# Routing turns and global outputs on 128 partitions, and the router's logits from one operand of both gate parts

## The chip, the cores and the metric

The kernel runs on one core of one Trainium2 chip. The metric is the device time of one execution, in microseconds (us); lower is better. Three executions of the kernel before took 813.44, 819.76 and 821.40 us, median 819.76.

## The reference

Three stages follow each other, in float32. Attention has 4 batches of 8 heads with 64 columns each: 32 global queries see all 544 keys (32 global, 512 local), and 512 local queries see the global keys and those at most 32 places away. The result, 4 x 544 = 2176 tokens of 512 columns, goes through a channel mix: each token is mixed with the one before it by `mu_k` and by `mu_r`, then `k = relu(xk @ w_k)`, `y = sigmoid(xr @ w_r) * (k*k @ w_v)`. Last comes a mixture of 8 experts:

```
logits = y @ w_gate                    # 8 columns
local  = sigmoid(y @ w_local)          # 1 column
e[s]   = argmax(logits[s]) if s == 0 or local[s] < 0.5 else e[s-1]
out[s] = softmax(logits[s])[e[s]] * (relu(y[s] @ w1[e[s]]) @ w2[e[s]])
```

The choice of an expert can be carried on from token to token within a batch, so it is a scan along the tokens.

## The kernel before

Phase 1 makes attention, channel mix and routing; phase 2 runs the experts. Most products are made with both operands split in two parts, an upper one and a rest (`mm3`, lines 19 to 24): upper by upper, upper by rest, rest by upper, three products added up in PSUM.

Attention goes by 16 units, pairs of heads, four to a batch. The first four units take float32 unsplit. `item` handles 128 local queries; `gitem` (lines 248 to 297) the 2 x 32 global ones of a unit. `gitem` ends with the products into `avg` (64 partitions x 128), a copy by ScalarE to `og` (line 287), a turn (a transpose on TensorE, that is a product with the identity `ident`) of the 64 x 128 values into `avt` (line 290), and two small copies by VectorE to `xT` (line 294), from which the channel mix reads.

The channel mix goes by nine groups of tokens, eight of two tiles of 128 tokens and one of one tile: 17 tiles. `run` (line 503) gives out the products `psk`, `psr` and `psv`. For each tile, `logits` (line 540) then makes four turns (`psy`), splits them in two parts `yT`, and multiplies with the gate: `s.g` holds `w_gate` (8 columns), `w_local` (1 column) and a column of zeros, halved, in an upper and a lower part, each 128 x 4 x 10 (`load_consts`, line 376). Four chunks of three products are 12 products into `psl`, 10 partitions x 128 tokens. ScalarE copies them to `lt` (10 x 128, line 560), TensorE turns them into `pslt` (128 x 10, line 564), VectorE copies them to `L` (line 567).

For each group, `route` (line 577) finds the expert of each token. It turns the codes of the tokens into a row on one partition (`psr1`, line 596), scans along the row (`row`, 1 x 256, line 600), turns the row back, tile by tile (`psc`, 1 x 128 to 128 x 1, line 609), and goes on on 128 partitions: counts, places in the experts' lists, and the lists (`psL`).

What sets the order: `Sched` (line 40) plans phase 1 when the program is built. Each stream of work yields steps with an engine, an assumed time (`yield op("P",.67,...)`: TensorE, 0.67 us), places to take and to leave, and a priority; instructions are given out in the order in which the steps start in that plan. The framework then orders the instructions by a simulated timeline of its own, so that the 12 products of one tile can stand apart in the trace. In the last groups some products for the first expert (`ahead`, line 791) are tied behind numbered steps of the last tile's routing (`step`, `order`, lists `ND` and `V7`). Phase 2 has a fixed order by hand.

At the start GpSimd fills constants and the tiles that must hold zeros (`pl`, `pg`, lines 97 and 98), before its first copies for attention (line 175).

Of the kernel before, what the change touches and what calls it, by code (L numbers as in the profile page):

```python
# [14 lines left out]
NEG=-1e9  # L15
FRESH=-1.08674975e-07  # the largest float32 z with 1/(1+exp(-z)) < 0.5 in float32
LEAST=float(np.array(0x38000000,np.int32).view(np.float32))  # the upper word of 2**-127 in float64, read as a float32

def mm3(nc,out,wh,wl,xh,xl,first,last,order=None):
    """out += w^T x with both operands split in two 12 bit parts"""  # L20
    i=nc.tensor.matmul(out,wh,xh,start=first,stop=False)  # L21
    if order: order(i)
    nc.tensor.matmul(out,wh,xl,start=False,stop=False)  # L23
    return nc.tensor.matmul(out,wl,xh,start=False,stop=last)  # L24


# order of the work: priorities of streams (the lower, the more urgent)
N0=3; PE0=-1.5; PC=-1; PW=1.5; PV=2; PM=0.5
NF=4  # the first pairs of heads, taken in float32 as it is
EV={"kn":"A","qn":"D","g":"D",0:"A",1:"A",2:"A",3:"A"}  # what empties their products' places  # L30
LN=12 ; PL=5  # parts of the experts' weights that are split in phase 1, and from which on GpSimd does it
GA=6; PA=6  # the group after which the first expert's first tile is closed, and the urgency of its work
ND=[k for k,n in enumerate([1, 5, 5, 11, 3, 4, 6, 16]) for _ in range(n)]  # how many of that tile's products follow each step of the last tile's routing
V7=[1,1,2,2,3,3,3,3]  # steps of the routing before the last tile's products
PP=(0,0,0,1,0,0,0,1); TW=(1,1,1,(2,4,6),3)  # parts of weights that GpSimd splits; where others go within a window of one tile
NR=4; NP=4  # places
FX=(1,3,5,7); FW=(2,4,6); NW=(2,3); NST=2  # where other work goes within a window; more stages for loads
LAT=0.2; DLAT=2.1; SLACK=dict(P=0.15,A=0,D=0,G=0)  # from an engine's end to the next step's start, and a load's
def op(e,d,need=(),free=(),when=None): return e,d,need,free,when
def wait(f): return "",0.0,(),(),f  # L40
class Sched:
    """The order in which the engines' instructions are given out. Streams of work are generators:
    each yields its next step (engine, time, places it takes, places it leaves, condition) and gives the
    step's instructions out when it is resumed, which is when the engine is free, the stream's step
    before is through and the places are there; of the streams that could go, the most urgent goes."""
# [7 lines left out]
    def one(s):  # L53
        """starts a step, if one can start now"""
        for x in sorted(s.L,key=lambda x:(s.t<x[3]+(SLACK.get(x[2][0],0) if x[4] else 0),x[0])):
            e,d,need,free,when=x[2]
# [20 lines left out]
class Pools:  # L77
    """a pool for the places of one tag and one for the others"""
# [4 lines left out]
class Attn:  # L83
    """attention by pairs of heads. The products of the first units, for whose time the tensor engine has
    nothing else to do, take float32 as it is; those of the others take it in two parts"""
    def __init__(s,tc,ident,mask,q_l,k_l,v_l,q_g,k_g,v_g,xT,sb,ps):
# [8 lines left out]
        s.pg=sb.tile([64,608],F32,name="pg",bufs=1)  # L95
        nc.vector.memset(s.gn,0.0)
        for t in s.pt_: nc.gpsimd.memset(t,0.0)
        nc.gpsimd.memset(s.pg,0.0)
        s.V={}; s.nat=set(); s.vnat=set(); s.T={}; s.sdone={}; s.vdone={}; s.odone={}
    def places(s,t):  # L100
        """of every other of the first units, in a tile that is filled later"""
        s.kwe=t[:,:896].rearrange("p (w i c) -> p w i c",w=1,i=4); s.gTe=t[:,896:992].unsqueeze(1); s.qTe=t[:,1024:1536].unsqueeze(1)
    def early(s,u): return u<NF
    def parts(s,u): return ((0,0),) if s.early(u) else ((0,0),(0,1),(1,0))
    def split(s,u,engine,out,x,place,d):
        """x to out, or to the two parts of it"""
# [53 lines left out]
    def prep(s,u,name):  # L160
        """transposed and split q or k of a pair of heads"""
# [33 lines left out]
    def item(s,u,i):  # L195
        """a block of local queries of a pair: its keys are the 32 before it, its own, the global ones
        and the 32 after it; the first block has none before it and the last one none after"""
# [27 lines left out]
        for c in range(2):  # L225
            # the second time with 32 of the first, for which v has zeros
            for h in range(2):
                nc.tensor.transpose(pt[:,c,h],p[:,h,c*96:c*96+P],s.ident)  # L228
# [15 lines left out]
    def weights(s,u):  # L244
        """a place for transposed weights or their parts"""
        return [s.sb.tile([P,2,256],F32 if s.early(u) else F32R,tag=t,name=t,bufs=2) for t in ("ph","plo")[:2-s.early(u)]]
    def v(s,u,w,i,c): return s.V[u][0][:,i,c] if s.early(u) else s.V[u][i//2][:,w,i%2,c]
    def gitem(s,u):
        """the global queries of a pair"""
# [36 lines left out]
        og=s.sb.tile([64,P],F32,tag="og",name="og",bufs=1)  # L286
        nc.scalar.activation(og,o,AF.Copy)
        yield op("P",.06,("av",))
        t=s.ps.tile([P,512],F32,tag="av",name="avt",bufs=1)[:,:64]
        nc.tensor.transpose(t,og,s.ident[:64,:64])  # L290
# [31 lines left out]
def band(nc,const):  # L322
    """0 for the keys in reach of a query of a block, NEG for the others"""
    m=const.tile([P,224],F32,name="mask")
    nc.gpsimd.memset(m,0.0)
    def keep(lo,hi,base,cm,step):
        # keeps 0 where base+cm*p+step*c >= 0
# [5 lines left out]
class Mix:  # L333
    """channel mix of groups of tokens, their router's logits and their places in the experts' lists"""
    def __init__(s,tc,ident,const,wsb,place,early,sb,ps,xT,mu,wk,wv,wr,gate,y):
# [7 lines left out]
        # places of the weights as they come: of other weights and of the router's operands, which are used later  # L343
# [7 lines left out]
    def consts(s,const):  # L351
# [11 lines left out]
        for b in range(NB):  # L363
            # 1 where p+128*c == 544*b
# [3 lines left out]
        # column m sums the rows p < m  # L368
# [3 lines left out]
        # of the first expert without its first tile  # L372
        s.up=t([P,E],"up"); nc.gpsimd.memset(s.up,float(P-1)); nc.gpsimd.memset(s.up[:,0:1],-1.0)
        s.last=t([1,1],"last"); nc.vector.memset(s.last,0.0)
        s.const=t
    def load_consts(s):
# [5 lines left out]
        g=t([P,4,10],"gf"); s.g=[t([P,4,10],f"g{w}",F32R) for w in range(2)]  # L382
# [4 lines left out]
        nc.vector.tensor_copy(s.g[0],g); nc.vector.tensor_sub(s.g[1],g,s.g[0].bitcast(F32))  # L387
    def weight(s,k,i):
        """loads 512 columns of a row, 128 of each of the four rows of wk or one row of the others,
        converts them from the bits of float64 and splits them"""  # L390
# [8 lines left out]
                # the least exponent is that of 2**-127 in float64  # L399
# [22 lines left out]
    def mixes(s,sched,groups):  # L422
        """mixed columns of tokens, split, group after group"""
# [42 lines left out]
    def kproc1(s,ps,kh,kl,b):  # L466
        """the same of a half of a group of one tile, which comes with the tokens on the partitions"""
# [28 lines left out]
    def run(s,sched,groups):  # L496
        """the groups of tokens one after another"""
# [41 lines left out]
    def logits(s,g,j,t,r,N):  # L539
# [14 lines left out]
        yield op("P",.67,(tag,),("yT",))  # L554
        ps=s.rps("psl",tag)
        for d in range(4): i=mm3(nc,ps[:10,:P],s.g[0][:,d],s.g[1][:,d],yT[0][:,d],yT[1][:,d],d==0,d==3)
        s.step(t,i)
        yield op("A",.16,(),(tag,))
        lt=s.sb.tile([10,P],F32,tag="lt",name="lt",bufs=1)
        nc.scalar.activation(lt,ps[:10,:P],AF.Copy)  # L560
        tag=s.ltag
        yield op("P",.05,(tag,))
        pl=s.rps("pslt",tag)[:,:10]
        s.step(t,nc.tensor.transpose(pl,lt,s.ident[:10,:10]))
        yield op("D",.1,(),(tag,))
        if g not in s.L: s.L[g]=s.sb.tile([P,N,10],F32,tag="L",name="L",bufs=2)
        nc.vector.tensor_copy(s.L[g][:,j],pl)
        yield wait(None)
        s.Lmade[g]+=1
    def routes(s,sched,groups):  # L570
        """the groups one after another; the last one's steps go before those that are left of the group before"""
# [5 lines left out]
    def route(s,g,tiles):  # L577
# [9 lines left out]
        # 8+8*token+8-expert at the tokens that choose, 0 at the others  # L587
# [11 lines left out]
        row=pool.tile([1,256],F32,tag="row",name="row",bufs=1)  # L599
# [4 lines left out]
        # p of each expert  # L604
        for j in range(N): nc.scalar.activation(ex[:,j],lg[:,j],AF.Exp,bias=nmx[:,j:j+1],scale=1.0,accum_out=sums[:,j:j+1])
        tag=s.rtag
        yield op("P",.05,(tag,))
        ps=s.rps("psc",tag)
        for j in range(N): i=nc.tensor.transpose(ps[:,j:j+1],row[:,j*P:(j+1)*P],s.ident[:1,:1])
# [413 lines left out]
```

## Time and profile before

| what | value |
|---|---|
| three timed runs | 813.44, 819.76, 821.40 us; median 819.76 |
| profiled execution | span 814.9 us from its first to its last instruction; the page gives no time of its own beside the span |
| TensorE (PE) busy | 747.8 us, 92% of the span, 4790 products |
| VectorE (DVE), ScalarE (ACT), GpSimd (POOL) busy | 525.7, 391.7, 388.1 us |
| chain that ended last | PE 69%, DVE 12%, DMA 8% |
| mean granted clock of TensorE | 0.956 of full |
| phase 1, phase 2 | to about 550 us; from there to the end |

How to read it: one execution was recorded. PE stands for products (MATMUL), PEld for loads of the operand that stays in the array. Products overlap, so the length of one (0.2 to 0.4 us) is not what it costs in a stream; that is the distance from its start to the start of the next. A line such as `L564` is a line of the kernel before, and `pslt<-ident,lt` names what is written and what is read. The form `10*128 10x10` reads: 10 rows by 128 columns in the array, 10 x 10 values stream through.

### The profile page before, as it was taken

What the parts mean: (1) busy time and instruction counts of PE and PEld (TensorE: products, weight loads), DVE (VectorE), ACT (ScalarE), POOL (GpSimd) and SP (SyncE); (2) the same over time, 40 slices, a digit from 0 to 9 for tenths busy, and PEclk for the clock granted to TensorE, in tenths of its full rate; (3) what the DMA queues carried; (4) which work ended last, traced back from release to release, by engine and by line L of the source; (5) the groups of instructions that cost most, each with busy time, mean ns of one, the idle gap of its engine ahead of it and who ended that gap; (6) DMA issues with size and microseconds to landing.
All of it is one profiled execution on the core that took longest, in us unless ns stands there. A gap on an engine that the chain in (4) does not pass through costs nothing.

```text
span 814.9 us, 14252 instructions
## 1 busy us (share of the span) xinstructions
PE 747.8 (92%) x4790; PEld 629.0 (77%) x4790; DVE 525.7 (65%) x1477; ACT 391.7 (48%) x978; POOL 388.1 (48%) x507
## 2 busy tenths in 40 slices
PE   6988899899999998999998999786899999999974
PEld 3655687798878877978887897565697999988963
DVE  6699889776695875786667845863473725536531
ACT  4787576663555644656544332213561615224420
POOL 6678868646153563462461412944462413324130
PEclk9997999999999999899998999978899999999988
DMA  6664241202102202111002200337684533518210
GB/s 151 168 183 147 74 113 54 76 22 54 35 15 76 50 13 70 44 27 50 23 14 99 96 27 27 117 121 227 212 270 158 165 122 111 198 40 272 85 54 7
DMA packets 93965, 78.71 MB, mean 97 GB/s; under 512 B 70558, under 2 KB 74654, under 8 KB 93858
## 3 DMA queue, kind: packets, MB, share of 16 engines
q1 hardware_dynamic: 89202, 63.23, 26.1%
q0 software_dynamic: 4240, 13.11, 4.8%
q10 hardware_dynamic: 416, 1.05, 0.4%
q8 instruction: 54, 0.88, 0.4%
q14 instruction: 53, 0.43, 0.2%
HBM read 68.44 MB, written 9.70 MB: 96 GB/s over the span
## 4 chain that ended last, share of the span: by engine, by line
PE 69%; DVE 12%; DMA 8%; ACT 3%; POOL 2%; issue 2%; SPq 2%; POOLq 0%; DVEq 0%; ACTq 0%
DMA xs<-y,idx 5%; PE av L236 4%; PE psk L21 4%; PE psk L23 4%; PE psk L24 4%; PE po L24 4%; PE po L21 4%; PE po L23 4%; PE psv L21 3%; PE psv L24 3%; PE psv L23 3%; PE ph L23 3%; PE ph L21 3%; PE ph L24 3%; PE ptp L228 3%
## 5 line engine op out<-in xcount | busy, mean ns | idle before, releaser
L222 POOL TENSOR_SCALAR pl<-pl,mx 128x192 f32<-128x192 f32 (+1 forms) x128 | 67.0, 536 | 73.4 <-DVE mx L219 39.6
L21 PE MATMUL psk<-xs,slot0h 128*128 128x256 f32 x256 | 75.5, 300 | 0.9 <-ACT xs L448 0.8
L216 ACT ACTIVATE pl<-pl,mx 128x224 f32<-128x224 f32 (+1 forms) x128 | 58.8, 461 | 36.2 <-DVE mx L213 31.3
L23 PE MATMUL psk<-xs,slot0h 128*128 128x256 f32 x256 | 74.4, 291 | 0.0
L24 PE MATMUL psk<-xs,slot0l 128*128 128x256 f32 x256 | 74.2, 291 | 0.0
L922 POOL DMA_INDIRECT out_dram<-osb,idx x19 | 23.5, 1236 | 97.1 <-DVE osb L921 81.9
L450 POOL TENSOR_TENSOR xs<-xm,xs 128x512 fp32r<-128x512 f32 (+1 forms) x36 | 46.2, 1292 | 43.7 <-ACT xs L448 43.7
L856 POOL DMA_INDIRECT xs<-y,idx x32 | 37.0, 1155 | 53.6 <-PE pt L863 39.2
L877 ACT ACTIVATE hh<-ph 128x256 fp32r<-128x256 f32 x56 | 21.6, 385 | 84.2 <-PE ph L24 83.0
L443 POOL TENSOR_SCALAR xm<-xT,mut 128x256 f32<-128x256 f32 (+7 forms) x96 | 43.2, 467 | 30.0 <-DVE xT L294 16.6
L21 PE MATMUL psv<-slot1h,kh 128*128 128x512 f32 x136 | 54.9, 405 | 0.0
L23 PE MATMUL psv<-slot1l,kh 128*128 128x512 f32 x136 | 54.3, 401 | 0.3 <-POOL slot1l L417 0.3
L24 PE MATMUL psv<-slot1h,kl 128*128 128x512 f32 x136 | 54.2, 401 | 0.0
L21 PEld LDWEIGHTS psk<-xs,slot0h 128*128 128x128 f32 x256 | 49.6, 196 | 2.3 <-ACT xs L448 1.2
L23 PEld LDWEIGHTS psk<-xs,slot0h 128*128 128x128 f32 x256 | 50.0, 195 | 0.7
L24 PEld LDWEIGHTS psk<-xs,slot0l 128*128 128x128 f32 x256 | 49.8, 195 | 0.5
L228 PE MATMUL ptp<-ident,pl 128*128 128x128 f32 x256 | 44.1, 293 | 5.7 <-DVE qT L119 1.3
L236 PE MATMUL av<-ph,v 128*128 128x256 f32 x192 | 44.7, 292 | 2.4 <-DVE xT L294 1.0
L119 DVE TENSOR_TENSOR plo<-ptp,ph 128x512 fp32r<-128x512 f32 x48 | 32.8, 685 | 19.2 <-ACT ph L117 18.9
L878 DVE SCALAR_TENSOR_TENSOR hl<-ph,hh 128x256 fp32r<-128x256 f32 x56 | 23.7, 423 | 32.9 <-ACT hh L877 32.5
L446 DVE SCALAR_TENSOR_TENSOR xm<-xT,mut,xm 128x256 f32<-128x256 f32 (+7 forms) x96 | 41.1, 463 | 3.6 <-POOL xm L443 3.5
L228 PEld LDWEIGHTS ptp<-ident,pl 128*128 128x128 f32 x256 | 31.2, 149 | 12.4 <-POOL pl L222 4.2
(732 smaller groups left out, 2519.8 us busy)
## 6 DMA issues: line engine op xcount, KB each, us to landing
st<-in_moe_w_dram SPq DMA_DIRECT2D x44, 512.0 KB, 4.2
sw<-in_moe_w_dram SPq DMA_DIRECT2D x18, 512.0 KB, 4.2
y<-r SPq DMA_DIRECT2D x17, 256.0 KB, 2.0
qn<-in_q_l_dram SPq DMA_DIRECT2D x32, 128.0 KB, 3.1
kn<-in_k_l_dram SPq DMA_DIRECT2D x32, 128.0 KB, 2.9
earlyh<-in_moe_w_k_dram SPq DMA_DIRECT2D x8, 512.0 KB, 4.7
raw<-in_moe_w_v_dram SPq DMA_DIRECT2D x8, 512.0 KB, 3.6
vn<-in_v_l_dram SPq DMA_DIRECT2D x24, 96.0 KB, 2.2
```

The source lines that it names most:

```text
L21: i=nc.tensor.matmul(out,wh,xh,start=first,stop=False)
L23: nc.tensor.matmul(out,wh,xl,start=False,stop=False)
L24: return nc.tensor.matmul(out,wl,xh,start=False,stop=last)
L119: nc.vector.tensor_sub(out[1],x,out[0].bitcast(F32))
L216: nc.scalar.activation(p[:,h,ks],p[:,h,ks],AF.Exp,bias=mx[:,h:h+1],scale=-1.0,accum_out=mx[:,4+h:5+h])
L222: nc.gpsimd.tensor_scalar(out=p[:,h,ks],in0=p[:,h,ks],scalar1=mx[:,6+h:7+h],scalar2=0.0,op0=ALU.mult,op1=ALU.add)
L228: nc.tensor.transpose(pt[:,c,h],p[:,h,c*96:c*96+P],s.ident)
L236: nc.tensor.matmul(o,s.v(u,x,i,c),P_[y][:,c],start=c==m==0,stop=c==1 and m==len(parts)-1)
L443: nc.gpsimd.tensor_scalar(out=x[:,u,o:o+k],in0=s.xT[b][:,c,q:q+k],scalar1=m[:,1,c:c+1],scalar2=0.0,op0=ALU.mult,op1=ALU.add)
L446: nc.vector.scalar_tensor_tensor(out=x[:,u,o:o+k],in0=s.xT[b][:,c,1+q:1+q+k],scalar=m[:,0,c:c+1],in1=x[:,u,o:o+k],op0=ALU.mult,op1=ALU.add)
L450: nc.gpsimd.tensor_sub(xl[:,cs,:n],x[:,:,:n],xh[:,cs,:n].bitcast(F32))
L856: s.nc.gpsimd.indirect_dma_start(out=s.xs[i][:,j,:],out_offset=None,in_=s.y,in_offset=IndirectOffsetOnAxis(ap=s.idx[:,ch:ch+1],axis=0))
```

## The change

Three parts. First, the turns of `lt`, `row` and `og` are made on all 128 rows: the three tiles are kept for the whole run at 128 partitions, filled with zeros by GpSimd at the start, and only their first 20, 1 and 64 rows are written later; each turn is a full 128 x 128 one with the whole identity, and of its result only the needed columns are read. Second, the two parts of the gate stand side by side in one operand: `s.g[0]` = upper, lower; `s.g[1]` = upper, zeros; each 128 x 4 x 20. The upper part of `yT` meets `s.g[0]`, the rest meets `s.g[1]`: two products a chunk, 8 a tile, into 20 partitions; after the turn VectorE adds the two halves of the 20 columns (a reduction in place of the copy). Third, the assumed times of three steps in the plan follow: 0.67 to 0.47 for the products, 0.05 to 0.11 for the turn of the logits, 0.05 to 0.11 per tile for the turn back of the row. The rest of the diff takes comments out.

```diff
+        s.pg=...; s.og=sb.tile([P,P],F32,name="og",bufs=1)
+        nc.gpsimd.memset(s.pg,0.0); nc.gpsimd.memset(s.og,0.0)
...
-        og=s.sb.tile([64,P],F32,tag="og",name="og",bufs=1)
-        nc.scalar.activation(og,o,AF.Copy)
+        og=s.og
+        nc.scalar.activation(og[:64],o,AF.Copy)
         yield op("P",.06,("av",))
-        t=s.ps.tile([P,512],F32,tag="av",name="avt",bufs=1)[:,:64]
-        nc.tensor.transpose(t,og,s.ident[:64,:64])
+        t=s.ps.tile([P,512],F32,tag="av",name="avt",bufs=1)[:,:P]
+        nc.tensor.transpose(t,og,s.ident)
...
+        s.lt=t([P,P],"lt"); s.row=t([P,256],"row")
+        for a in (s.lt,s.row): nc.gpsimd.memset(a,0.0)
...
-        g=t([P,4,10],"gf"); s.g=[t([P,4,10],f"g{w}",F32R) for w in range(2)]
+        g=t([P,4,10],"gf"); gz=t([P,4,10],"gz"); s.g=[t([P,4,20],f"g{w}",F32R) for w in range(2)]
...
-        nc.vector.tensor_copy(s.g[0],g); nc.vector.tensor_sub(s.g[1],g,s.g[0].bitcast(F32))
+        nc.vector.memset(gz,0.0)
+        for w in range(2): nc.vector.tensor_copy(s.g[w][:,:,0:10],g)
+        nc.vector.tensor_sub(s.g[0][:,:,10:20],g,s.g[0][:,:,0:10].bitcast(F32)); nc.vector.tensor_copy(s.g[1][:,:,10:20],gz)
...
-        yield op("P",.67,(tag,),("yT",))
+        yield op("P",.47,(tag,),("yT",))
-        for d in range(4): i=mm3(nc,ps[:10,:P],s.g[0][:,d],s.g[1][:,d],yT[0][:,d],yT[1][:,d],d==0,d==3)
+        for d in range(4):
+            for w in range(2): i=nc.tensor.matmul(ps[:20,:P],s.g[w][:,d],yT[w][:,d],start=d==w==0,stop=d==3 and w==1)
...
-        lt=s.sb.tile([10,P],F32,tag="lt",name="lt",bufs=1)
-        nc.scalar.activation(lt,ps[:10,:P],AF.Copy)
+        nc.scalar.activation(s.lt[:20],ps[:20,:P],AF.Copy)
-        yield op("P",.05,(tag,))
-        pl=s.rps("pslt",tag)[:,:10]
-        s.step(t,nc.tensor.transpose(pl,lt,s.ident[:10,:10]))
+        yield op("P",.11,(tag,))
+        pl=s.rps("pslt",tag)[:,:P]
+        s.step(t,nc.tensor.transpose(pl,s.lt,s.ident))
-        nc.vector.tensor_copy(s.L[g][:,j],pl)
+        nc.vector.tensor_reduce(out=s.L[g][:,j],in_=pl[:,:20].rearrange("p (q e) -> p e q",q=2),axis=X,op=ALU.add)
...
-        row=pool.tile([1,256],F32,tag="row",name="row",bufs=1)
+        row=s.row[0:1]
-        yield op("P",.05,(tag,))
+        yield op("P",.11*N,(tag,))
-        for j in range(N): i=nc.tensor.transpose(ps[:,j:j+1],row[:,j*P:(j+1)*P],s.ident[:1,:1])
+        for j in range(N): i=nc.tensor.transpose(ps[:,j*P:(j+1)*P],s.row[:,j*P:(j+1)*P],s.ident)
-        ei=sm("ei",dt=I32); nc.vector.tensor_scalar(out=ei,in0=ps[:,:N],scalar1=-1.0,...)
+        ei=sm("ei",dt=I32); nc.vector.tensor_scalar(out=ei,in0=ps[:,0:n:P],scalar1=-1.0,...)
```

## Rows read from the trace of the kernel before

**Rows 1.** Busy time by stretch: stretch, length, busy time (instructions) per engine, clock, DMA
```profile
0.00:95.00 95.00, 75.76 (x377) 52.04 (x377) 78.95 (x245) 65.71 (x197) 70.52 (x118) 0.91 0.55 148
95.00:515.00 420.00, 405.88 (x2871) 346.81 (x2871) 302.31 (x987) 220.77 (x611) 203.64 (x313) 0.98 0.18 50
```

**Rows 2.** The page: shares of the chain that ended last, by engine
```profile
PE 69%; DVE 12%; DMA 8%; ACT 3%; POOL 2%; issue 2%; SPq 2%; POOLq 0%; DVEq 0%; ACTq 0%
```

**Rows 3.** Timeline of PE (start, length, instruction): products of the logits, and of `avg`
```profile
164.28 0.23 PE L21 MATMUL psl<-yT,g 128*10 128x128 f32 x1
164.59 0.22 PE L24 MATMUL psl<-yT,g 128*10 128x128 f32 x1
...
437.12 0.23 PE L283 MATMUL avg<-v,plo 128*64 128x128 f32 x1
437.30 0.23 PE L283 MATMUL avg<-v,plo 128*64 128x128 f32 x1
```

**Rows 4.** Timeline of PE: a turn of the logits in a stream of `psk`
```profile
167.93 0.28 PE L23 MATMUL psk<-xs,slot0h 128*128 128x256 f32 x1
168.05 0.28 PE L24 MATMUL psk<-xs,slot0l 128*128 128x256 f32 x1
168.26 0.23 PE L564 MATMUL pslt<-ident,lt 10*128 10x10 f32 x1
...
168.64 0.28 PE L23 MATMUL psk<-xs,slot0h 128*128 128x256 f32 x1
```

**Rows 5.** Timeline of PE: a full 128-row turn in a stream of `psk`
```profile
165.17 0.28 PE L23 MATMUL psk<-xs,slot0h 128*128 128x256 f32 x1
165.29 0.27 PE L228 MATMUL ptp<-ident,pl 128*128 128x128 f32 x1
...
165.52 0.28 PE L21 MATMUL psk<-xs,slot0h 128*128 128x256 f32 x1
```

**Rows 6.** Timeline of PE: the two turns of a group's row in a stream of `psk`
```profile
343.77 0.28 PE L24 MATMUL psk<-xs,slot0l 128*128 128x256 f32 x1
343.97 0.28 PE L609 MATMUL psc<-ident,row 1*128 1x1 f32 x2
...
344.40 0.28 PE L23 MATMUL psk<-xs,slot0h 128*128 128x256 f32 x1
```

**Rows 7.** Timeline of PE: a turn of `og` in a stream of `psv`; `psv` undisturbed
```profile
250.12 0.39 PE L23 MATMUL psv<-slot1l,kh 128*128 128x512 f32 x1
250.44 0.27 PE L290 MATMUL avt<-ident,og 64*128 64x64 f32 x1
...
250.97 0.39 PE L21 MATMUL psv<-slot1h,kh 128*128 128x512 f32 x1
...
504.63 0.40 PE L23 MATMUL psv<-slot1l,kh 128*128 128x512 f32 x1
504.87 0.39 PE L24 MATMUL psv<-slot1h,kl 128*128 128x512 f32 x1
```

**Rows 8.** Timeline of GpSimd and VectorE at the start
```profile
0.80 0.20 POOL masks.py:197 MEMSET ident<- 128x128 f32 x1 [0.29 <-POOLq L1010]
...
7.73 0.51 POOL L175 TENSOR_SCALAR kw<-kw 128x96 f32<-128x96 f32 x2 [0.64 <-ACT kw L111]
```

**Rows 9.** Timeline of VectorE and GpSimd at the routing of the last group but one
```profile
520.83 0.17 DVE L584 TENSOR_REDUCE mx__6938<-L 128x2 f32<-128x16 f32 x1
520.91 5.87 DVE L585 SCALAR_TENSOR_TENSOR fr<-L,first 128x2 f32<-128x2 f32 x1
527.11 3.41 DVE L590 SCALAR_TENSOR_TENSOR fe<-fe,base,fr 128x1 f32<-128x1 f32 x2
...
525.74 1.03 POOL L773 TENSOR_SCALAR slot1h<-st 128x1024 fp32r<-128x1024 f32 x1
```

**Rows 10.** Busy time by stretch, around a fall of the granted clock
```profile
322.60:326.20 3.60, 1.46 (x10) 1.13 (x10) 3.52 (x20) 1.83 (x9) 2.74 (x4) 1.00 0.19 44
326.20:333.00 6.80, 6.80 (x31) 5.88 (x30) 4.63 (x24) 4.47 (x16) 5.19 (x9) 0.50 0.18 40
```

## The prediction of the time after

> **What bounds the kernel now.** I read the busy time by stretch first, because the change touches phase 1 alone and phase 1 has stages with different limits. Up to 95 us TensorE (PE) works 75.76 us of 95; VectorE 78.95 and GpSimd 70.52 are about as full, so no engine alone sets the pace there. From 95 to 515 us PE works 405.88 of 420 us, VectorE 302.31, ScalarE and GpSimd less [rows 1]: this stretch is bound by PE, which stands idle for 14.1 us in all. The chain that ended last runs over PE for 69% of the whole span [rows 2]. In such a stretch an edit is worth what it takes out of PE's queue. The length of a product in the trace does not tell that, since products overlap; so I went to the timeline of PE and took distances between starts, around each thing that the change touches. The last view is the timeline of the end of phase 1, where PE waits for the routing: there the length of a chain counts, not the work.
>
> **The logits' products.** In one tile six of the twelve start within 164.28 and 164.59 us, five distances, 0.062 us each [rows 3]. The operand that is loaded grows from 10 to 20 columns; products with 64 columns loaded and the same 128 streamed start 0.18/3 = 0.060 us apart [rows 3], so 20 columns cost no more than 10. Four products fewer on each of 17 tiles: 17 x 4 x 0.06 = 4.1 us.
>
> **The turn of the logits.** Undisturbed, one `psk` follows another after 0.12 us. From the `psk` before the turn to the second `psk` behind it pass 168.64 - 168.05 = 0.59 us, which hold two `psk` and the turn: the turn costs 0.59 - 0.24 = 0.35 us [rows 4]. The gap stands before it (0.21 instead of 0.12) and in the products behind it, though only 10 values a row stream through. A full turn of 128 rows in the same kind of stream costs 0.35 - 0.24 = 0.11 us [rows 5]. The new turn has exactly that form. Gain 0.24 x 17 = 4.1 us.
>
> By the Trainium skill (TensorE: Matmul & The Clock Gate, section "Back-to-back issue gap") a product of 1 to 64 columns takes about 60 cycles and one of 128 columns 134. By that rule the widened turn would cost 74 cycles more, an estimate of 0.03 us at 2.4 GHz, and this part would lose 17 x 0.03 = 0.5 us instead of winning 4.1. The rows speak against it here: the small turn holds up its neighbours and the full one does not.
>
> **The turns back of the row.** Two of them between `psk` take 344.40 - 343.77 - 0.24 = 0.39 us [rows 6]; two full turns would take 0.22 [rows 5]. Eight groups of two tiles win 0.17 each, the last group about half of it: 1.5 us.
>
> **The global outputs.** Between `psv`, which follow each other after 0.24 us, a turn of 64 rows costs 250.97 - 250.12 - 0.48 = 0.37 us [rows 7], a full one 0.11: 0.26 us. There are 16, one to a unit; the four of the first batch fall before 95 us, where PE is not the bound, and I count them at nothing. 12 x 0.26 = 3.1 us.
>
> **What is added.** GpSimd fills three more tiles at the start: two like the identity at 0.20 us, and one twice as wide, up to 0.40. These 0.8 us stand before its first copy for attention, before which it waits 0.64 us for ScalarE [rows 8]; so 0 to 0.2 us is late for the first scores. VectorE gets three more small instructions when the gate is loaded, at most 0.17 us each like a short reduction [rows 9], 0 to 0.5 us, in a stretch where it is full for 79 of 95 us; I take 0.2 for both together. The reduction in place of the copy to `L` costs between nothing and a whole instruction of 0.17 us; VectorE has room from 95 to 515 us, and what counts is the last tile: 0.2 at most. The copies to `lt` and `og` keep their length. The change adds no DMA and no wait of a new kind; the tiles that are now kept were single places before, so the next copy to `lt` still waits for the turn of the last.
>
> **The sum.** Out of PE's queue go 4.1 + 4.1 + 1.5 + 3.1 = 12.8 us. How much of it reaches the end lies between the share of the chain on PE, 0.69 [rows 2], and PE's busy share in the stretch, 405.88/420 = 0.97 [rows 1]; I take 0.8, 10.2 us. The part that is lost goes into waits of PE for VectorE's and ScalarE's steps of attention, which are late next. Less 0.4 us for what is added, 9.8 us. The span of 814.9 becomes 805.1. The median of the runs, 819.76, lies 4.9 us above that span, and the runs lie up to 8 us apart; I put the gain on the median: **810 us**. With 0.6 to 1.0 of the 12.8 us this case by itself reaches from 807 to 812.5.
>
> **Rivals.** *The freed time turns into waits.* The plan of phase 1 is made anew with other assumed times, and attention's chain over VectorE, ScalarE and GpSimd paces it. For it: there are places where PE idles in the middle of the stretch, such as 322.6 to 326.2 us, with 1.46 of 3.6 us busy while VectorE is full [rows 10]. Against it: such places make up 14.1 us of 420 only [rows 1]. With a third of the 12.8 us left, the time is 815.5. Chance 0.18.
>
> *The full turns are no cheaper* (the change does not do what it says): the 0.35 us belong to a turn that waits for ScalarE's copy and not to its few rows. Then only the four products count, 4.1 x 0.8 = 3.3 us, and the time is 816.5. Against it: the full turn in rows 5 comes from other engines' work too and costs 0.11. Chance 0.07. By the rule of the Trainium skill cited above (same page and section) the 17 + 17 + 12 turns would even cost 0.03 us more each, an estimate of 1.4 us, and the time would be 818 us.
>
> *The routing's waits behind GpSimd at the end of phase 1.* For the last group but one, two instructions of VectorE with two operands in SBUF took 5.87 and 3.41 us where they need about 0.2; the first ended at 526.78 us, when a row of GpSimd's splits of weights ended (525.74 + 1.03) [rows 9]. PE and the last tile wait for them. If the new order lets the routing through before that, some 8 us go as well: 802, chance 0.06. If the last group meets such a row too, 9 us come on top: 819, chance 0.05.
>
> *Slower: the clock.* From 326.2 to 333.0 us PE ran at half its clock, 1.2 GHz, after the stretch in which it was busy for 1.46 of 3.6 us [rows 10]. What is done there in 6.8 us takes 3.4 at the full clock, so each such fall costs 3.4 us. If the freed time is not used but stands as gaps of that kind, nothing is won, and each gap brings a fall. Up to two further falls stay within 1%; three are 10.2 us, and it decides from there: 830 us. For it: 12.8 us of gaps are room for several of them. Against it: the whole stretch has a mean clock of 0.98 [rows 1], and the gaps would have to gather at a few places. Chance 0.09.
>
> **How the numbers follow.** The forecast keeps 0.55. A measurement of this kernel can tell about 1%, 8.2 us, from no change; that is 811.6 us. Four fifths of the forecast's own range lie below it, 0.44; with the 0.06 of a freed end of phase 1 it is 0.50 for faster. Within 1% fall the rest of the forecast (0.11), the lost gain (0.18), the turns that keep their price (0.07) and the second wait behind GpSimd (0.05): 0.41. Slower: 0.09. The range goes from 802, the freed end, to 820, which takes in the cases of a lost gain, of dear turns and of the second wait; outside stay the clock's case and what the runs scatter.
>
> **What would show it.** Starts of the eight products 0.06 us apart and 8 x 17 = 136 of them; the turns of the logits, of the row and of `og` at 0.11 us between two products of a stream, with no gap before or behind; PE's work up to the routing of the last tile shorter by 12 to 13 us, and its idle time in the bound stretch still near 14 us. The prediction is wrong if that idle time has grown by as much as the work has shrunk (the waits), if the gaps around the turns stay (the price of the turns), or if the difference sits behind 515 us, at the waits for GpSimd or in further stretches at half clock.

## The result, and the profile after

The changed kernel takes 825.80 us (median of 11 runs, 822.67 to 829.38), the kernel before 815.48 us in the same measurement (11 runs, 812.05 to 821.40): a ratio of 1.0113, 95% interval 1.0088 to 1.0138. It is slower by 10 us; a gain of 9.8 us was forecast, from a median of three runs (819.76 us) that 11 runs put 4.3 us lower. The profiled execution has a span of 827.6 us, 12.7 more than that of before, and is the slowest of its 11 runs.

The instructions did become cheaper. Timeline of PE after (start, length, instruction): seven of the eight products of one tile's logits, the two turns of a row, a turn of `og` among `psv`, a turn of the logits among `psk`. Everything behind the new fills stands 1 to 7 lines lower than before (L571 was L564, L291 was L290, L616 was L609).

```profile
156.46 0.62 PE L564 MATMUL psl<-rt,g 128*20 128x128 f32 x7
...
181.72 0.28 PE L24 MATMUL psk<-xs,slot0l 128*128 128x256 f32 x1
181.84 0.38 PE L616 MATMUL psc<-ident,row 128*128 128x128 f32 x2
181.98 0.48 PE L21 MATMUL psr<-wrh,xs 128*128 128x512 f32 x1
182.30 0.40 PE L23 MATMUL psr<-wrl,xs 128*128 128x512 f32 x1
...
243.98 0.40 PE L23 MATMUL psv<-slot1l,kh 128*128 128x512 f32 x1
244.21 0.27 PE L291 MATMUL avt<-ident,og 128*128 128x128 f32 x1
244.24 0.47 PE L24 MATMUL psv<-slot1h,kl 128*128 128x512 f32 x1
244.55 0.39 PE L21 MATMUL psv<-slot1h,kh 128*128 128x512 f32 x1
...
274.48 0.28 PE L23 MATMUL psk<-xs,slot0h 128*128 128x256 f32 x1
274.60 0.27 PE L571 MATMUL pslt<-ident,lt 128*128 128x128 f32 x1
274.62 0.36 PE L24 MATMUL psk<-xs,slot0l 128*128 128x256 f32 x1
274.82 0.28 PE L21 MATMUL psk<-xs,slot0h 128*128 128x256 f32 x1
```

From 274.48 to 274.82 us pass 0.34 us, of which two `psk` are 0.24: the turn costs 0.10, where it was 0.35 [rows 4]. The turn of `og` costs 0.57 - 0.48 = 0.09, where it was 0.37 [rows 7]. From the `psk` ahead of the two turns of a row to the second `psr` behind them (it starts at 182.30) pass 0.58 us, which hold a `psk` of 0.12 and a `psr` of 0.23: the two cost 0.23, where they cost 0.39 [rows 6]. The products of the logits now load 20 columns; the seven shown last 0.62 us together and 0.22 each, so they start 0.07 us apart (0.06 was predicted). PE has 4722 products instead of 4790.

The time went elsewhere. Busy time by stretch after (stretch, length, busy time of PE, PEld, VectorE, ScalarE and GpSimd with instructions, granted clock, DMA), to be held against the second line of [rows 1]:

```profile
95.00:515.00 420.00, 400.12 (x2780) 341.61 (x2779) 297.30 (x977) 219.25 (x608) 199.91 (x310) 0.96 0.18 49
```

In the stretch that PE binds it now idles for 19.9 of 420 us instead of 14.1, and the granted clock is 0.96 instead of 0.98. Then the end of phase 1: VectorE and GpSimd (POOL) at the routing of the last group but one (`fr`, `fe`, `cnt`, `ri` and `rt` are small tiles of the routing), and what PE waits for (us in all, times, longest).

```profile
526.59 9.79 DVE L592 SCALAR_TENSOR_TENSOR fr<-L,first 128x2 f32<-128x2 f32 x1
536.70 0.35 DVE L597 SCALAR_TENSOR_TENSOR fe<-fe,base,fr 128x1 f32<-128x1 f32 x2
544.07 1.78 DVE L642 TENSOR_TENSOR cnt<-cnt,oh 128x8 bf16<-128x8 bf16 x1
545.85 2.31 DVE L637 CAST ri<-rk 128x2 int32<-128x2 f32 x1
```
```profile
526.36 1.06 POOL L780 TENSOR_SCALAR slot1h<-st 128x1024 fp32r<-128x1024 f32 x1
527.38 2.38 POOL L786 TENSOR_TENSOR slot0l<-st,slot0h 128x1024 fp32r<-128x1024 f32 x1
529.72 1.04 POOL L780 TENSOR_SCALAR slot1h<-st 128x1024 fp32r<-128x1024 f32 x1
530.73 4.62 POOL L786 TENSOR_TENSOR slot1l<-st,slot1h 128x1024 fp32r<-128x1024 f32 x2
535.33 1.03 POOL L780 TENSOR_SCALAR slot1h<-st 128x1024 fp32r<-128x1024 f32 x1
542.42 1.05 POOL L780 TENSOR_SCALAR slot1h<-st 128x1024 fp32r<-128x1024 f32 x1 [6.06 <-DMA st<-in_moe_w_dram]
543.44 4.71 POOL L786 TENSOR_TENSOR slot1l<-st,slot1h 128x1024 fp32r<-128x1024 f32 x2
```
```profile
PE psr L603 <- DVE fe L597: 7.5, 1, 7.5
PE psL L653 <- DVE rt L649: 3.3, 1, 3.3
```

L592 is the L585 of [rows 9]. It ended at 536.38 us, when GpSimd's row of splits ended (535.33 + 1.03). Before, the splits had another order with a pause of 0.39 us behind L773, and L585 got through there after 5.87 us. Now there is no pause for nine microseconds, and a second row from 542.42 on holds up two more instructions. PE waits 10.8 us at these two places. Before, the same view (515 to 551 us) had:

```profile
PE psr L596 <- DVE fe L590: 6.2, 2, 4.3
PE psL L646 <- DVE rt L642: 0.3, 1, 0.3
```

Against before, the profiled execution is 5.6 us late at the turn of the logits of the last tile but one (525.98 against 520.36), 9.8 at phase 2's first gather (557.85 against 548.03; the load of the tokens that an expert gets), 12.7 at the end.

### The profile page after: what moved, and what is told of

Its sections match the earlier page's. It is cut to its first block, busy times and chain, and to the rows that moved or that the text cites. A ratio compares the mean times of both kernels' runs of the same rounds, so it can differ in the third digit from the quotient of the medians.

```text
span 827.6 us, 14120 instructions
## 1 busy us (share of the span) xinstructions
PE 745.4 (90%) x4722; PEld 627.6 (76%) x4722; DVE 529.3 (64%) x1480; ACT 393.1 (48%) x978; POOL 387.1 (47%) x510
## 4 chain that ended last, share of the span: by engine, by line
PE 67%; DVE 15%; DMA 8%; ACT 3%; issue 2%; SPq 2%; POOL 1%; DVEq 0%; ACTq 0%; POOLq 0%
DMA xs<-y,idx 6%; PE av L236 4%; PE psk L21 4%; PE psk L24 3%; PE psk L23 3%; PE po L21 3%; PE po L24 3%; PE po L23 3%; PE psv L23 3%; PE psv L21 3%; PE ph L23 3%; PE psv L24 3%; PE ph L24 3%; PE ph L21 3%; PE ptp L228 2%
## 5 line engine op out<-in xcount | busy, mean ns | idle before, releaser
L222 POOL TENSOR_SCALAR pl<-pl,mx 128x192 f32<-128x192 f32 (+1 forms) x128 | 64.2, 514 | 90.1 <-DVE mx L219 35.1
L453 DVE SCALAR_TENSOR_TENSOR xm<-xT,mut,xm 128x256 f32<-128x256 f32 (+7 forms) x96 | 45.4, 507 | 5.7 <-POOL xm L450 5.5
L228 PEld LDWEIGHTS ptp<-ident,pl 128*128 128x128 f32 x256 | 30.2, 144 | 12.8 <-DVE ph L114 2.1
```

The lines of the kernel that those rows point to most:

```text
L222: nc.gpsimd.tensor_scalar(out=p[:,h,ks],in0=p[:,h,ks],scalar1=mx[:,6+h:7+h],scalar2=0.0,op0=ALU.mult,op1=ALU.add)
L453: nc.vector.scalar_tensor_tensor(out=x[:,u,o:o+k],in0=s.xT[b][:,c,1+q:1+q+k],scalar=m[:,0,c:c+1],in1=x[:,u,o:o+k],op0=ALU.mult,op1=ALU.add)
```

## The experiments

The framework orders the engines' instructions anew whenever an instruction or an assumed time changes. Counted on the two traces, by what the instructions write and read and with the products of the logits left out, the longest series that keeps the order of before holds 2109 of TensorE's 3202 instructions of phase 1 in the changed kernel, and 858 of the 1312 of VectorE that both have. So the first question was whether the new instructions lose the time or the new order. To hold an order, every call of phase 1 is recorded, and each instruction is tied behind the one that preceded it on its engine in the kernel before, with no semaphore added. In kernels with a held order all these instructions show the recorder's line, L981, L985 or L988.

```diff
+        for a,b in zip(at,at[1:]):   # at: the order in the kernel before, as places in the recorded list L
+            tc.add_manual_dep(L[b].ins,L[a].ins.name,DependencyInfo(NoSync,SCHED_ONLY))
-            m=phase1(tc,st,ins,...)
+            log={...}; m=phase1(Tc(tc,log),st,ins,...); fixed(tc,log)
```

All were timed in five rounds against the kernel before (815.7 to 817.0 us, 17 to 35 runs). The last column is (1 - granted clock) x span, the mean over the runs; for the kernel before it is 31.5 to 31.8 us, for the changed kernel 39.6. It tells about what the spells at half clock cost where PE works through them. The splits that e6 to e9 and e11 do without are named below.

| run | us | ratio, 95% interval | clock column |
|---|---|---|---|
| e1 changed, TensorE's order held | 820.3 | 1.0040, 1.0022 to 1.0057 | 37.6 |
| e2 before, TensorE's order held | 816.6 | 0.9983, 0.9951 to 1.0015 | 30.8 |
| e3 changed, old assumed times | 815.9 | 0.9984, 0.9960 to 1.0007 | 35.4 |
| e4 before, new assumed times | 817.6 | 1.0013, 0.9987 to 1.0039 | 34.1 |
| e5 changed, all orders held | 813.0 | 0.9953, 0.9921 to 0.9985 | 33.5 |
| e6 before, no late GpSimd splits | 808.6 | 0.9919, 0.9891 to 0.9946 | 26.5 |
| e7 changed, all orders held, no late splits | 808.1 | 0.9905, 0.9869 to 0.9940 | 30.0 |
| e8 changed, no late splits | 814.5 | 0.9988, 0.9962 to 1.0014 | 32.1 |
| e9 changed, old times, no late splits | 807.5 | 0.9882, 0.9853 to 0.9912 | 29.5 |
| e10 before, three more fills | 815.9 | 0.9986, 0.9957 to 1.0014 | 28.6 |
| e11 full turns only, orders held, no late splits | 806.7 | 0.9884, 0.9849 to 0.9919 | 25.4 |
| e12 before, another assumed time for `psy` | 823.8 | 1.0091, 1.0059 to 1.0122 | 34.4 |

**The order of TensorE, the assumed times (e1 to e4).** e1 and e2 hold TensorE's order in the changed kernel (with the old assumed times, as in e5, e7 and e11) and in the kernel before. e3 and e4 exchange the assumed times:

```diff
-        yield op("P",.47,(tag,),("yT",))    # e3; e4 has the opposite in the kernel before
+        yield op("P",.67,(tag,),("yT",))
-        yield op("P",.11,(tag,))
+        yield op("P",.05,(tag,))
-        yield op("P",.11*N,(tag,))
+        yield op("P",.05,(tag,))
```

> The changed kernel, with TensorE's instructions of phase 1 held in the order that they have in the kernel before (the list of the before's 3113 instructions; the other engines follow it and stand nearly as before). Theory 1 (the instructions became cheaper as forecast, and the newly planned order of phase 1 ate it in waits and clock falls): 9 us off the kernel before, so a ratio of 0.987 to 0.992, about 806 us. Theory 2 (the new instructions cost more than they look: the zeros, the copies in front of the full turns, the routing's two-operand additions): as slow as the changed kernel, a ratio of 1.009 to 1.014, about 825 us.

> Control: the kernel before, with TensorE's instructions of phase 1 held in their own order by the same means. Both theories: a ratio of 0.998 to 1.002. If holding the order costs something by itself, it shows here.

> The changed kernel with the three times that the planner assumes (.47, .11, .11 a part) put back to the before's (.67, .05, .05); nothing else. If the three assumed times alone made the loss: 0.987 to 0.992, about 806 us. If the order also moves because there are other instructions to be ordered (theory 1 in its wide form): anywhere from 0.99 to 1.015, with PE's idle time in phase 1 going along with the time. Theory 2: 1.009 to 1.014.

> The kernel before with the three assumed times of the changed kernel and none of its instructions: TensorE's phase 1 is in another order, and does the same work. Theory 1: a loss, 1.003 to 1.02, since an order alone can cost what was seen. Theory 2: 0.998 to 1.002, the order is nothing.

Holding the order costs nothing that can be measured (e2). e1 fits neither theory. With the products in the same order, the two traces can be laid one on the other: PE is late by 4.7 us at the fourth turn of `og` (99.38 against 94.65 in the kernel before), has won all of that back at the turn of the last tile but one (520.35 against 520.36), and loses again at the routing, where VectorE stands behind GpSimd as in the changed kernel:

```profile
520.96 9.88 DVE L592 SCALAR_TENSOR_TENSOR fr<-L,first 128x2 f32<-128x2 f32 x1
```

The order of the other engines, which e1 leaves free, had changed, most of all at the start. The assumed times alone make the loss neither way: taken back they win 10 us (e3 against the changed kernel), put into the kernel before they cost nothing that can be measured (e4). The routing does not tell e3 from the changed kernel: in e3 PE has the same two waits of 7.5 and 3.3 us there, and from the turn of the last tile but one to phase 2's first gather pass 32.0 us in e3, 31.9 in the changed kernel and 27.7 before. Their difference lies ahead of it: e3 reaches that turn at 515.02 us, the changed kernel at 525.98.

**All orders, and GpSimd's splits (e5 to e8).** e5 holds the order of all five engines. The edit of e6, e7 and e8 lets ScalarE and VectorE make the last seven parts of the first expert's split weights:

```diff
-LN=12 ; PL=5
+LN=12 ; PL=12
```

> The changed kernel with all five engines in the order of the kernel before (the new fills and the three new small instructions of VectorE are left free). Found so far, from the run with TensorE's order held: PE lost some 4 us up to 95 us, won 6 us back between 95 and 519 us, and lost 4 to 6 us at the routing of the last groups, where VectorE's two-operand instructions waited for the end of a row of GpSimd's splits. Theory O (order alone): the start and the end become those of the kernel before, all of the gain stays, a ratio of 0.988 to 0.992. Theory W (a wall: the routing of group 7 goes on when GpSimd's row of splits ends, at about 529 us, however early PE gets there): the first gain is lost at the wall, 0.995 to 1.000. Theory F (the new fills and copies cost time themselves at the start): PE is still late by 3 us or more at 100 us, 0.998 to 1.005.

> The kernel before with the last seven parts of the first expert's weights split by ScalarE and VectorE instead of GpSimd (the limit PL from 5 to 12): TensorE's order is the same but for 10 of 3113 instructions. Theory W: the waits of 5.9 and 3.4 us of VectorE in the routing of group 7 go, PE waits some 4 us less there, a ratio of 0.993 to 0.997. If the wall costs PE nothing, because the last tile's products have to wait for the first expert's weights anyway: 0.998 to 1.002, and VectorE's additional 8 us of splits may make it 1.003.

> Both: the changed kernel in the order of the kernel before, and the last seven parts split by ScalarE and VectorE. Theory W: the gain of the middle reaches the end, and the wall's own 4 us go too: 0.982 to 0.990, 802 to 809 us. Theory O: as the run with all orders held, less what the kernel before gains by the same edit. Theory F: 0.992 to 1.0.

> The changed kernel as it is, newly planned, with the last seven parts split by ScalarE and VectorE. In its trace VectorE stood 9.8 us behind GpSimd in the routing of group 7 and 4 us behind it later, and PE waited 7.5 us. Theory W: 7 to 9 us less than the changed kernel, 817 to 819 us, a ratio to the kernel before of 1.000 to 1.004. If the loss of the changed kernel is all in its order further up: 1.009 to 1.013 as it was.

In the order of before the changed kernel is faster than the kernel before, by 0.2 to 0.8%; newly ordered it is slower by 0.9 to 1.4%. The order alone is worth 13 us (825.8 - 813.0). The start is no longer late in e5 (94.68 us at the fourth turn of `og`), so the fills and copies themselves cost nothing there: theory F falls. e5 falls into the range of theory W, but not by its mechanism. Its end of phase 1 (VectorE, then GpSimd with the first gather of phase 2):

```profile
515.82 6.59 DVE L988 SCALAR_TENSOR_TENSOR fr<-L,first 128x2 f32<-128x2 f32 x1
522.73 3.36 DVE L988 SCALAR_TENSOR_TENSOR fe<-fe,base,fr 128x1 f32<-128x1 f32 x2
```
```profile
522.73 1.05 POOL L988 TENSOR_SCALAR slot1h<-st 128x1024 fp32r<-128x1024 f32 x1 [0.34 <-DMA st<-in_moe_w_dram]
...
543.48 1.01 POOL L863 DMA_INDIRECT xs<-y,idx  x1 [8.84 <-DVE cint L988]
```

The row of splits does not end at a fixed time: it begins when PE is through with `psk`, and moved forward with PE. The routing still waits as long as before, and 4.5 us of gain reach phase 2 (543.48 against 548.03); at the end of the trace 3.2 are left (811.7 against 814.9). What the row costs is seen in e6, where the same two instructions take 0.15 and 0.34 us and PE no longer waits for `fe` at all:

```profile
526.76 0.15 DVE L585 SCALAR_TENSOR_TENSOR fr<-L,first 128x2 f32<-128x2 f32 x1
529.02 0.34 DVE L590 SCALAR_TENSOR_TENSOR fe<-fe,base,fr 128x1 f32<-128x1 f32 x2
```

e6 wins 7 us, more than the wait of 6.2 us, of which I had expected 2.4 to 5.7. The clock adds to it. Busy time by stretch, the kernel before and e6:

```profile
515.00:551.00 36.00, 28.53 (x150) 21.94 (x149) 25.61 (x95) 6.54 (x17) 23.01 (x16) 0.86 0.38 126
```
```profile
515.00:551.00 36.00, 32.07 (x195) 25.25 (x193) 27.15 (x109) 14.98 (x29) 10.88 (x8) 1.00 0.51 154
```

Behind the wait PE ran at half its clock for 10.2 us before (from 527.6 us); without the wait the clock is full through the whole stretch. In the traces this part, from the turn of the last tile but one to the first gather, is 9.1 us shorter in e6 (18.6 against 27.7 us), though e6 comes to it 5.9 us later (526.21 against 520.36). In the changed kernel the same edit wins 11.3 us (e8), where theory W had 7 to 9.

e7 missed. Its trace shows PE 8.0 us ahead of e6 at the turn of the last tile but one (518.23 against 526.21 us), but its time is not measurably below that of e6. (The profiled run of e6 took 813.3 us and that of e7 812.4, 4 to 5 us above their medians.) At phase 2's first gather e7 is still 5.5 us ahead (539.33 against 544.83), at the end 0.9 (810.7 against 811.6): most of the lead goes in phase 2. On the way PE waits 2.0 us for `rt` where e6 waits 0.3, and the runs' clock column is 3.4 us above that of e6. Which gap brings the lower clock is not settled.

**Further draws, and the turns alone (e9 to e12).**

```diff
+        nc.gpsimd.memset(s.pt_[0][:,0,:P],0.0)                                  # e10, in Attn
+        nc.gpsimd.memset(s.ones,1.0); nc.gpsimd.memset(s.i136,0.0); ...iota(s.i136,...)  # e10, in the constants
...
-            for w in range(2): i=nc.tensor.matmul(ps[:20,:P],s.g[w][:,d],yT[w][:,d],...)  # e11
+            i=mm3(nc,ps[:10,:P],s.g[0][:,d],s.g[1][:,d],yT[0][:,d],yT[1][:,d],d==0,d==3)
...
-        yield op("P",.44,(tag,),(),lambda: t in s.ymade)                        # e12
+        yield op("P",.5,(tag,),(),lambda: t in s.ymade)
```

> The changed kernel with the three assumed times of the kernel before, and the last seven parts of weights split by ScalarE and VectorE: no order is held. With GpSimd's splits in place PE was 5 us ahead of the kernel before at 515 us and lost all of it in the routing of the last groups. Theory W (the wall): those 5 us stay, and the wall's own waits and half-clock spell go, 0.984 to 0.990, 803 to 808 us. If what is won is given back further on, in phase 2 or to the clock: 0.990 to 0.996, and the granted clock is below that of the kernel before with the same edit (0.967).

> The kernel before with three more fills by GpSimd at the start, of the size and in the place of the changed kernel's, which nothing uses (and one line of constants made again): the instructions after them are ordered anew, 1824 of TensorE's 3113 stand in the order of before. If the fills are what makes the start of the changed kernel late, by the order that follows from them: PE late by 3 us or more from 40 to 150 us, a ratio of 1.003 to 1.010. If not: 0.998 to 1.002.

> Of the change only the full turns (12 products a tile as before), all engines in the order of the kernel before, the last seven parts split by ScalarE and VectorE: to be read against the two runs with that edit, the kernel before (PE passes the turn of the last tile but one at 520.8 us) and the whole change (8.1 us earlier). By the prediction's prices the turns are 8.7 of 12.8 us, so some 5.5 us earlier there. If the turns win nothing and the products all: under 1 us earlier.

> The kernel before with one assumed time changed that has nothing to do with the change (the four turns of y, .44 to .5): the same instructions in another order, 2272 of TensorE's 3113 in the order of before. If an order is a draw with some microseconds of scatter: outside 0.997 to 1.003, to either side. If orders of one plan are as good as each other: inside.

e12 settles what an order can do by itself: one assumed time of a step that this change does not touch, from .44 to .5, costs the kernel before 7 us, with the same instructions. e10 and e4 are two other draws, which cost nothing; the fills do not make the start late by themselves (e10 is 1.7 us early at the fourth turn of `og`, 92.94 us). e9 and e11 are as fast as anything here, 1.2% below the kernel before; their intervals overlap with those of e6 and e7. With the splits moved, the change is worth from a loss of 6 us (e8 against e6) to a gain of 3 us (e9 against e6), according to its order, and no more than that is settled. e11 missed its number: its trace is 11.2 us ahead of e6 at the turn of the last tile but one (515.03 us), more than the whole change (e7, 8.0). It was 2.5 us ahead at the fourth turn of `og` already (93.82 against 96.36) and has less time at half clock, so a lead in one trace is no measure of what the turns save.

The stretch that PE binds, from the fourth turn of `og` (near 95 us) to the turn of the logits of the last tile but one (before, changed, e1, e3, e5, e12; then e6, e7, e11):

```profile
94.65:520.36 425.71, 411.52 (x2910) 351.20 (x2909) 304.83 (x993) 223.07 (x616) 209.14 (x317) 0.98 0.19 52
95.31:525.98 430.67, 410.79 (x2846) 350.55 (x2846) 304.02 (x994) 223.57 (x615) 209.30 (x315) 0.96 0.19 51
99.38:520.35 420.97, 404.91 (x2848) 349.25 (x2847) 303.67 (x993) 221.92 (x616) 207.85 (x316) 0.97 0.19 52
96.31:515.02 418.71, 403.88 (x2848) 347.32 (x2847) 303.89 (x994) 222.79 (x616) 208.62 (x317) 0.98 0.19 52
94.68:515.21 420.53, 403.35 (x2847) 347.58 (x2846) 306.45 (x993) 222.40 (x616) 208.70 (x316) 0.98 0.19 52
95.45:528.00 432.55, 415.98 (x2911) 351.83 (x2910) 305.76 (x993) 224.79 (x615) 211.68 (x316) 0.98 0.19 51
96.36:526.21 429.85, 414.43 (x2914) 353.33 (x2914) 306.10 (x996) 226.43 (x621) 202.55 (x312) 0.97 0.19 53
95.51:518.23 422.72, 405.03 (x2848) 348.71 (x2846) 306.88 (x996) 225.97 (x620) 203.46 (x313) 0.97 0.19 53
93.82:515.03 421.21, 406.21 (x2912) 350.41 (x2910) 306.22 (x996) 225.79 (x620) 202.57 (x313) 0.98 0.19 54
```

At half clock `psk` start 0.21 us apart (before, 444.76, 444.97 and 445.18 us) instead of 0.12, near double. So, as an estimate, I take half of the time that the trace gives at half clock off the busy time:

| | length | PE idle | at half clock | work at full clock |
|---|---|---|---|---|
| before | 425.7 | 14.2 | 17.1 | 403.0 |
| changed | 430.7 | 19.9 | 30.3 | 395.6 |
| e1 | 421.0 | 16.1 | 23.9 | 393.0 |
| e3 | 418.7 | 14.8 | 13.7 | 397.1 |
| e5 | 420.5 | 17.2 | 20.5 | 393.1 |
| e12 | 432.6 | 16.6 | 20.5 | 405.7 |
| e6 | 429.9 | 15.4 | 23.9 | 402.5 |
| e7 | 422.7 | 17.7 | 23.9 | 393.1 |
| e11 | 421.2 | 15.0 | 17.1 | 397.7 |

In the order of before the change takes 9.9 us of work from PE (e5; 10.0 in e1, 9.9 in e7); e11, which has the same order, splits it into 5.3 for the turns and 4.6 for the products. Of these 9.9 us 3.0 came back as idle time and 1.7 as time at half clock, so e5 is 5.2 us ahead there. In the changed kernel as it is the work fell by 7.3, the idle time grew by 5.7 and half clock cost another 6.6: 5.0 us late, and 0.7 it was late before. In another order the same products give another sum, by up to 4 us (e5 and e3; before and e12), so work is to be compared within one order.

## Why the prediction was wrong

**The prices were right in a stream, and not all turns stand in one.** Of the 12.8 us that were to leave PE's queue 9.9 did, up to the last tile: 4.6 for the products, where 4.1 was predicted for the whole run, and 5.3 for the turns, where 8.7 was. Laid one on the other, e6 and e7 give the difference around single turns: a median of 0.20 us for the logits (11 turns; 0.24 was predicted), 0.18 for a group's row (6; 0.17), 0.27 for `og` (10; 0.26), where two of the ten won nothing. But a turn that stands beside the products of attention on 64 rows (`s<-kw,qT`) wins nothing: the time from the product ahead of it to the second start behind it is 0.31 and 0.29 us around one turn of the logits (at 326.58 us in e6, 321.22 in e7), 0.48 and 0.49 around one of `og` (115.62, 114.91), 0.63 and 0.64 around the two of a row, here in e6 and e7:

```profile
407.29 0.28 PE L24 MATMUL psk<-xs,slot0l 128*128 128x256 f32 x1
407.50 0.28 PE L609 MATMUL psc<-ident,row 1*128 1x1 f32 x2
...
407.92 0.27 PE L207 MATMUL s__5482<-kw,qT 64*128 64x224 f32 x1
```
```profile
400.46 0.28 PE L988 MATMUL psk<-xs,slot0l 128*128 128x256 f32 x1
400.58 0.38 PE L988 MATMUL psc<-ident,row 128*128 128x128 f32 x2
...
401.10 0.27 PE L988 MATMUL s__5429<-kw,qT 64*128 64x224 f32 x1
```

This speaks for a price of changing the number of rows from one product to the next, which beside such products is paid in any case.

That the full turns would be no cheaper is refuted. The Trainium skill (TensorE: Matmul & The Clock Gate, section "Back-to-back issue gap") has more cycles for 128 columns than for 64 or fewer, for a product by itself; for these turns in a stream the trace does not agree, the wider turn is the cheaper one. By the Trainium skill (TensorEngine Tiling (Array Packing), section "Key Properties") a change of the array's tiling mode drains TensorE. The rows fit that in sign, with 0.2 to 0.3 us for a turn of 10 or 64 rows and 0.09 for one of a single row over a full one; that such a turn changes the mode is not shown, and the page gives no figure.

**What was added cost nothing that can be seen, where 0.4 us was predicted.** In e5 the three fills took 0.19, 0.19 and 0.30 us and disappeared in GpSimd's wait for ScalarE: the first copy for attention began at 7.62 us, at 7.73 before [rows 8].

**The step that failed is the sum.** Four fifths of the work taken out were to reach the end, a share chosen between PE's share of the chain (0.69) and its busy share (0.97), as if the work stayed in its order and PE's waits and clock stayed as they were. That failed twice. The new order has a price of its own, for which the forecast had no term; it stood only in the rivals, as a gain that is lost (815.5 us), a second row of splits (819) and gaps at half clock (830). With the same instructions the order was worth 13 us (e5 against the changed kernel), and an edit that has nothing to do with this one draws an order that costs 7 us (e12). That a step's assumed time became truer was no protection. And in the order of before not four fifths but a third or so reached the end: 3 to 4 of 9.9 us (e5, by the medians and by the ratio). There the first rival's mechanism shows, waits of PE in the place of the freed time (3.0 us), and half clock (1.7). Why the changed kernel's order is worse than that of e3 is known only as idle time and half clock (5.1 us more idle, 16.6 more at half clock, in the stretch that PE binds), not as one wait.

**The rival at the routing came true, in other numbers.** At 819 us it had the last group meet another row of GpSimd's splits. A second row did come, but it held the last group but one again (its forms are two columns wide, the last group's one), for 1.78 and 2.31 us, with the last group's first instructions queued behind; and before that the same group stood behind an unbroken row for 9.79 us. PE's waits grew from 6.5 to 10.8 us there, about the 4.2 us that the profile loses between the turn of the last tile but one and phase 2. e1 and e3 lose as much there (32.2 and 32.0 us against 27.7), so it is a part of the loss and not the whole. e8 shows the price of all these waits: 11.3 us go with the splits. I had treated them as something that may or may not move; they cost the kernel before 7 us too (e6), and were the better edit. The prediction also read the 3.41 us of [rows 9] as one instruction that waits for a row; they are two, of 1.09 and 2.39 us (last section).

**The rival of the clock was right in its mechanism.** The clock column rose from 31.5 to 39.6 us, by 8 us where 10 were lost, in single spells: in the bound stretch the trace of the changed kernel has spells of 6.8, 10.2 and 6.8 us from 231.4, 327.0 and 354.3 us and the end of one from 91.5, the trace of before 6.8, 3.4 and 6.8 us from 326.2 [rows 10], 394.5 and 442.2. It was priced as freed time that stands as gaps; in fact the half clock went with the order (30.3 us of it in the bound stretch of the changed kernel, 13.7 in e3, with the same instructions) and, at the routing, with the rows of GpSimd.

**Left open.** 2.9 us of the profile's loss stand in phase 2, whose code is the same. PE waits there once, near 780 to 800 us, for nothing that the profile shows (changed, then before; us in all, times, longest):

```profile
PE pht L21 <- issue: 6.0, 1, 6.0
PE pht L21 <- issue: 4.3, 1, 4.3
```

This is more than scatter: the wait is 5.7 to 6.2 us in all seven traces with eight products a tile and 4.2 to 4.9 in all seven with twelve, among them e11, which has the full turns (4.7). So about 1.4 us come back here with the gate's new operand, out of the 4.6 that its products save. What PE waits for, and where the rest of the 2.9 us goes, stays open.

## What to carry to other kernels

When a planner orders the program, an edit has two effects: its own and a new draw of the order; hold the old order for one run, or change something unrelated for another, and the two come apart. Before taking work from the bound engine, look at its longest waits: one edit at a wait of 6 us won 7 us here, 9.9 us of removed work 3 to 4 in the order of before. A wait of the bound engine costs twice if its clock falls behind it. And price an instruction by its neighbours: the same turn saved 0.27 us in one place and nothing in another.

## What the runs showed of the hardware

While GpSimd works through a row of splits, VectorE's instructions with two operands in SBUF (the chip's memory that the engines read from) wait. `fr` waited until the row ended: 5.87 us over four of GpSimd's instructions before, 6.59 over four in e5, 9.79 over six in the changed kernel; without the row it took 0.15 us (e6). Others of this kind got through where two of GpSimd's instructions follow each other without a pause. Before, the first `fe` ended at 528.20 us, when a split ended (527.16 + 1.04), and the second at 530.52, when the next did (528.17 + 2.34); in the changed kernel `cnt` ended at 545.85 (544.07 + 1.78), when the first of two splits did (543.44 + 2.39):

```profile
527.11 1.09 DVE L590 SCALAR_TENSOR_TENSOR fe<-fe,base,fr 128x1 f32<-128x1 f32 x1
528.13 2.39 DVE L590 SCALAR_TENSOR_TENSOR fe<-fe,base,fr 128x1 f32<-128x1 f32 x1
527.16 1.04 POOL L773 TENSOR_SCALAR slot1h<-st 128x1024 fp32r<-128x1024 f32 x1 [0.39 <-DMA st<-in_moe_w_dram]
528.17 2.34 POOL L779 TENSOR_TENSOR slot1l<-st,slot1h 128x1024 fp32r<-128x1024 f32 x1
543.44 2.39 POOL L786 TENSOR_TENSOR slot1l<-st,slot1h 128x1024 fp32r<-128x1024 f32 x1
```

Why `fr` stays behind at borders at which these get through, no run shows. By the Trainium skill (SBUF — State Buffer, section "Who interferes with whom") a VectorE instruction with two inputs in SBUF contends with a GpSimd instruction that reads SBUF, through ports of which one of them has the exclusive use. The trace agrees that they exclude each other; that a wait lasts over several of GpSimd's instructions is more than the page says. A cast with one operand waited too, for 2.31 us.

A transpose of few rows among full products is dear: 0.35 us for 10 rows [rows 4] against 0.10 for all 128 with zeros below. Beside products on 64 rows the two cost the same.
